# The first piece of q through SyncE's queue in fp32, with a new written-out order, in a fused Nyström attention and feed-forward kernel

## The chip, the cores and the metric

One core of one Trainium2 chip runs the whole program in one launch. The metric is the device time of an execution in microseconds, lower is better. The engines are TensorE (PE, its weight loads PEld), VectorE (DVE), ScalarE (ACT), GpSimd (POOL) and SyncE (SP); DMAs are issued by GpSimd (software queue, q0 in the profile) and by SyncE (hardware queue, q1), and once by ScalarE.

## The reference

```python
# q, k, v: (8, 8, 576, 64) fp32; m = 32 landmarks, scale = 1/8
q_lm = q.reshape(B, H, 32, 18, 64).mean(axis=3)      # and k_lm from k
sm = lambda a, b: softmax(scale * a @ b.T)           # with +1e-9 in the divisor
A, Bm, C = sm(q, k_lm), sm(q_lm, k_lm), sm(q_lm, k)
Z = Bm.T / (norm1(Bm) * norminf(Bm) + 1e-6)          # of each head
for _ in range(6):
    Z = 2 * Z - Z @ Bm @ Z
x = (A @ Z @ C @ v), heads side by side               # (4608, 512)
out = relu(x @ w_in) ** 2 @ w_out                     # w_in 512x2048, w_out 2048x512
```

## The kernel before, in words

The work goes by batch b = 0..7. A batch has two tiles of heads: r = 0 is heads 0 to 3, r = 1 heads 4 to 7, with partition = (head, landmark) and 18 tokens of 64 values along a partition (1152 values). Names of operations end in the batch, then in what they handle: `ldq0.1` loads q of batch 0, heads 4 to 7.

**Loads.** `load_qk` (L411 to L417) issues a DMA from GpSimd that reads fp32 and writes bf16 into the tile X (three buffers). v, w_in and w_out come the same way. All loads are in one software queue, in the order of their words; at most eight are in flight, and GpSimd waits for the eighth last to land before it issues the next. SyncE issues only the stores of the output (L1095).

**Attention of a batch.** `lm` on PE sums the 18 tokens of each landmark (two forms: L492 for heads 0 to 3 of batch 0 and for batch 1, L499 for heads 4 to 7 of batch 0), from X with the identity `ident` as the weight; `lmc`, `lme` bring it into LM, `lmt` transposes. `T` (L461, DVE) transposes X in 32x32 blocks. `B` (L546) is the 32x32 score matrix of the landmarks; `Bmx Bsb Bex Bsu Brc Bml` are its softmax (Bml, L562, multiplies by the reciprocal into Bf), `Bmb` (L580) makes the bf16 copy Bb from the same factors, `Btr` transposes it, `Bcs Bnm Brn` give the norm, `BBT Yi Zi` (L643) start the iteration, `N` (PE) and `U` (DVE, L699) are its six steps. `SC` (L721), `Cmx`, `Cex` (L762), `CT` are C; `CR` gathers its sums through `cpick` (c11). `CV` is C times v (L807), `Zm` and `ZC` multiply by Z, `W` (L878) multiplies by w_in and `We` evicts it. `SA` is A for batches 0 and 1 (L927), whose softmax is `Amx` (L945), `Asb` (L948), `Aex` (L950), `Asu` (L952), `Arc` (L955) and `Aml` (L957, the multiplication by the reciprocal); for batch 0 each is cut in two, a and b. `Ap` transposes on PE and `Ab` evicts. `bk` (L933) spreads k's landmarks for SA.

**Feed-forward.** `F` (L1042) multiplies, `R` applies relu out of PSUM (L1056 on ACT, L1058 on DVE), `Q` squares (L1063 on ACT, L1065 on DVE or GpSimd) into the ring G, `O` (L1082) is the second product, `Oe` evicts and `St` stores.

**What sets the order.** Nothing is scheduled by the compiler: a string `ORDER` lists all 1421 operations by name, with the PSUM bank (`@2`) and, where it isn't the first choice, the engine (`/A` ACT, `/D` DVE, `/P` POOL). A planner (`Plan.schedule`) walks it with a cost for each operation and a free time for each engine (`T0`), a start of the software queue (`SW0`) and a landing delay (`LAND`), and the operations are emitted by planned start. So an engine's instruction order is that of the words given to it. `Plan.fillers` then puts products of constants (`onesb`, L1156) into PE's planned gaps until the first `O0.`, with a rule for how much of each stretch of 3.41 us has to be filled. Their results are not used.

Of the kernel before, what the change touches and what calls it, by code (L numbers as in the profile page):

```python
# [53 lines left out]
class Plan:  # L54
# [104 lines left out]
    def fillers(self, until, width, emit):  # L159
# [3 lines left out]
        for o in ops:  # L163
            a, b = o.start, o.start + o.engs["PE"]
            free = [j for j in range(8)
                    if all(h[1] >= a + 0.15 or h[2] <= at - 0.02 for h in self.history if h[0] == j)]
            if free:
                unit = width if at > 6 else 2 * width
                gaps.append([at, max(0, int((a - 0.05 - at) / unit)), free[0], a, unit])
            kind = o.name.rstrip("0123456789.ab")  # L170
            used.append((a, b, self.USE.get(kind, 0.95)))
            at = max(at, b + 0.04)

        def share(t):
# [12 lines left out]
        for at, n, j, _, unit in gaps:  # L187
# [5 lines left out]
            o.emit = lambda e, j=j, n=n: emit(j, n)  # L193
# [7 lines left out]
T0 = {"PE": 1.1, "ACT": 1.1, "DVE": 1.1, "POOL": 1.31, "SP": 1.1}  # L201
SW0, LAND, LOADED = 1.5, 1.75, 140.0
# [53 lines left out]
def kernel(  # L256
# [155 lines left out]
    def load_qk(b, t, r):  # L412
# [4 lines left out]
           W=[("X", b % 3, t, r)], nbytes=589824, queue="sw")  # L417
# [33 lines left out]
    def attention(b):  # L451
        x, tt, lm, lt = X[b % 3], TT[b % 2], LM[b % 2], LT[b % 2]
        kx = lambda t, r: ("X", b % 3, t, r)
# [5 lines left out]
        def transposes(t):  # L459
            for r in range(2):  # L460
# [3 lines left out]
                   R=[kx(t, r)], W=[kt(t, r)])  # L464
# [19 lines left out]
        def landmarks(rs):  # L484
# [4 lines left out]
            def lmx(e):  # L489
# [14 lines left out]
               R=["ident", *[kx(t, r) for t in range(2) for r in rs]], W=[pl_], alloc=[pl_],  # L504
# [37 lines left out]
        def sB(e):  # L542
# [19 lines left out]
        op(f"Bml{b}", {"DVE": 0.14}, lambda e: nc.vector.tensor_tensor(  # L562
            bf[:], bl[:], bc(s_[:, 4:6]), ALU.mult), R=[kb("bl"), kb("brc")], W=[kb("bf")])
# [15 lines left out]
        else:  # L579
            op(f"Bmb{b}", {"DVE": 0.14}, lambda e: nc.vector.tensor_tensor(  # L580
                bb[:], bl[:], bc(s_[:, 4:6]), ALU.mult), R=[kb("bl"), kb("brc")], W=[kb("bb")])
# [47 lines left out]
        def bbt(e):  # L629
# [281 lines left out]
        for u in range(2) if b in TOKENS else ():  # L911
# [28 lines left out]
            for j, (x0, x1) in enumerate(zip(cuts, cuts[1:])):  # L940
# [11 lines left out]
                op(f"Asu{b}.{u}{z}", {"DVE": v_(w)}, lambda e, s3=s3, sa3=sa3, at=at: nc.vector.tensor_reduce(  # L952
                    s3(1)[:, at], sa3[:, at], axis=AX.X, op=ALU.add), R=kx_("sa"), W=kx_("asu"))
                op(f"Arc{b}.{u}{z}", {"DVE": 0.07 + 0.0045 * (x1 - x0)}, lambda e, s3=s3, at=at:
                   nc.vector.reciprocal(s3(2)[:, at], s3(1)[:, at]), R=kx_("asu"), W=kx_("arc"))  # L955
                op(f"Aml{b}.{u}{z}", {"DVE": v_(w)}, lambda e, sa3=sa3, b3=b3, anv=anv, at=at:
                   nc.vector.tensor_tensor(anv.rearrange("p (x m) -> p x m", m=M)[:, at], sa3[:, at],  # L957
                                           b3(2)[:, at], ALU.mult),
                   R=[*kx_("sa"), *kx_("arc")], W=kx_("An"))
# [216 lines left out]
FLAT_LM = ((0, 0), (1, 0))  # L1176

# [142 lines left out]
```

## Time and profile before

| | |
|---|---|
| median of 3 runs | 264.09 us (263.49 to 264.58) |
| profiled execution | 264.03 us, span 262.3 us |
| instructions in the span | 7508 |
| mean granted TensorE clock | 0.998 |
| HBM read, written | 48.50 MB, 9.44 MB |

The time of an execution is about 1.7 us more than the span of the profile, which begins with the program's first instruction and ends with its last. In the profile "DMA X<-in_q_dram" names the transfer that writes tile X from q. Names of tiles leave out the buffer's number, so every load of q has that name, and they are told apart by their time. A line in brackets after an instruction is the idle time of its engine ahead of it and what ended it.

### The profile page before, as it was taken

The page shows a single profiled execution, that of the slowest core. Times are in us where ns is not written, and L with a number is a line of the kernel's source. Part 1 is how long each engine was busy: PE and PEld are TensorE (multiplying, and loading weights), DVE is VectorE, ACT ScalarE, POOL GpSimd, SP SyncE. Part 2 cuts the span into 40 slices and gives each one's busy share as a digit, 9 for nine tenths or more (in the row PEclk, how much of TensorE's full clock was granted, in tenths as well). Part 3 has the DMA queues.
Part 4 walks back from the last instruction along what each step waited for, and adds up shares of the span by engine and source line. Part 5 has one row for each costly group of instructions (what it writes and reads, how often), then busy time and mean ns, then how long its engine had stood idle before and what let it go on. Part 6 is the DMA issues. An engine that isn't in the chain of part 4 may idle for free.

```text
span 262.3 us, 7508 instructions
## 1 busy us (share of the span) xinstructions
PE 248.2 (95%) x3053; PEld 140.7 (54%) x3092; DVE 208.9 (80%) x551; ACT 184.6 (70%) x334; POOL 70.3 (27%) x114
## 2 busy tenths in 40 slices
PE   7797999999999999999999999899999999999993
PEld 2464566566454656465555456466454655457552
DVE  3899898888999798988998889979998868764110
ACT  1272797866498897898767389888676965699421
POOL 8446486554021442053601411000202010000000
PEclk9999999999999999999999999999999999999999
DMA  6999999999977399689997495360005210060045
GB/s 103 205 187 200 208 207 206 205 210 192 191 153 170 39 223 216 138 117 216 198 188 166 75 223 107 58 152 1 2 0 135 70 42 1 2 152 8 2 115 128
DMA packets 25123, 34.18 MB, mean 130 GB/s; under 512 B 2432, under 2 KB 14464, under 8 KB 25088
## 3 DMA queue, kind: packets, MB, share of 16 engines
q0 software_dynamic: 19168, 24.25, 55.3%
q1 hardware_dynamic: 5840, 9.38, 13.8%
q8 instruction: 24, 0.39, 0.6%
q14 instruction: 11, 0.09, 0.1%
q10 hardware_dynamic: 80, 0.07, 0.1%
HBM read 48.50 MB, written 9.44 MB: 221 GB/s over the span
## 4 chain that ended last, share of the span: by engine, by line
PE 64%; DVE 12%; ACT 8%; DMA 8%; issue 4%; POOL 2%; SPq 2%; POOLq 0%; DVEq 0%; ACTq 0%
PE ps L1082 35%; PE ps L1042 17%; DMA X<-in_q_dram 4%; DMA out_dram<-OS 4%; PE ps L878 3%; ACT RS L1056 2%; ACT G L1063 2%; PE ps L807 2%; SPq L1095 2%; PE ps L721 2%; POOL X L416 1%; DVE RS L1058 1%; DVE An L1012 1%; ACT C L762 1%; PE ps L477 1%
## 5 line engine op out<-in xcount | busy, mean ns | idle before, releaser
L1082 PE MATMUL ps<-w_out,G 128*128 128x512 bf16 (+1 forms) x557 | 133.9, 373 | 2.9 <-issue 1.4
L1082 PEld LDWEIGHTS <-G 128*128 128x128 bf16 x592 | 54.5, 98 | 54.4 <-issue 5.5
L1042 PE MATMUL ps<-AT,WP 128*128 128x288 bf16 (+2 forms) x512 | 74.6, 286 | 0.7 <-DVE RS L1058 0.2
L1056 ACT ACTIVATE RS<-ps 128x576 bf16<-128x576 f32 (+2 forms) x96 | 59.4, 652 | 11.2 <-PE ps L1042 7.3
L1042 PEld LDWEIGHTS <-WP 128*128 128x128 bf16 x512 | 48.1, 98 | 21.3 <-issue 2.9
L1063 ACT ACTIVATE G<-RS 128x576 bf16<-128x576 bf16 (+2 forms) x69 | 46.6, 690 | 4.0 <-DVE RS L1058 3.3
L403 ACT CAST WP<-ps 128x1024 bf16<-128x1024 f32 (+1 forms) x28 | 25.9, 971 | 9.1 <-PE ps L878 9.0
L403 ACT COPY OS<-ps 128x512 f32<-128x512 f32 (+2 forms) x32 | 18.0, 569 | 18.6 <-PE ps L1082 17.6
L1058 DVE TENSOR_SCALAR RS<-ps 128x576 bf16<-128x576 f32 (+2 forms) x32 | 24.1, 754 | 6.3 <-PE ps L1042 4.4
L622 POOL TENSOR_TENSOR BD<-ST,blkb 128x256 bf16<-128x256 bf16 x14 | 9.8, 702 | 68.7 <-DVE ST L699 57.3
L1065 DVE TENSOR_TENSOR G<-RS 128x576 bf16<-128x576 bf16 (+2 forms) x51 | 22.3, 451 | 7.2 <-ACT RS L1056 6.8
L461 DVE STREAM_TRANSPOSE TT<-X 128x576 uint32<-128x576 uint32 x32 | 24.3, 765 | 1.1 <-DMA X<-in_k_dram 0.5
L762 ACT ACTIVATE C<-ps,sm 128x576 bf16<-128x576 f32 x16 | 14.3, 906 | 7.8 <-DVE sm L759 7.8
L699 DVE SCALAR_TENSOR_TENSOR ST<-ST,ps 128x128 bf16<-128x128 bf16 (+1 forms) x48 | 12.8, 267 | 6.9 <-PE ps L685 4.9
L432 POOL DMA_DIRECT2D V<-in_v_dram x24 | 12.8, 534 | 13.3 <-PE ps L807 7.5
L407 DVE COPY OS<-ps 128x512 f32<-128x512 f32 (+1 forms) x6 | 3.8, 625 | 14.1 <-DMA out_dram<-OS 8.7
L1156 PE MATMUL ps<-onesb 128*128 128x512 bf16 (+1 forms) x38 | 11.9, 407 | 2.0 <-DVE onesb L339 1.5
L622 POOL TENSOR_TENSOR BD<-Bt,blkb 128x256 bf16<-128x256 bf16 x4 | 3.1, 770 | 36.6 <-ACT Bt L403 11.0
L759 DVE TENSOR_REDUCE sm<-ps 128x1 f32<-128x576 f32 x16 | 11.6, 745 | 0.7 <-PE ps L721 0.6
L1065 POOL TENSOR_TENSOR G<-RS 128x512 bf16<-128x512 bf16 (+1 forms) x8 | 8.8, 1100 | 7.5 <-ACT RS L1056 7.4
L995 DVE STREAM_TRANSPOSE SA<-ps 128x320 f32<-128x320 f32 (+1 forms) x24 | 10.0, 456 | 0.9 <-PE ps L716 0.7
L878 PE MATMUL ps<-w_in,ZC 64*32 64x512 bf16 x256 | 10.6, 383 | 0.0
(139 smaller groups left out, 299.9 us busy)
## 6 DMA issues: line engine op xcount, KB each, us to landing
out_dram<-OS SPq DMA_DIRECT2D x70, 128.0 KB, 2.4
X<-in_q_dram POOLq DMA_DIRECT2D x16, 288.0 KB, 9.5
X<-in_k_dram POOLq DMA_DIRECT2D x16, 288.0 KB, 8.6
XS<-in_q_dram POOLq DMA_DIRECT2D x5, 576.0 KB, 6.9
XS<-in_k_dram POOLq DMA_DIRECT2D x5, 576.0 KB, 10.4
V<-in_v_dram POOLq DMA_DIRECT2D x8, 288.0 KB, 9.2
w_in<-in_moe_w_in_dram POOLq DMA_DIRECT2D x8, 256.0 KB, 10.5
w_out<-in_moe_w_out_dram POOLq DMA_DIRECT2D x4, 512.0 KB, 9.3
```

Source lines behind the costliest of these rows:

```text
L403: nc.scalar.copy(o, i)
L432: lambda e, r=r, p0=p0, n=n, src=src: nc.gpsimd.dma_start(vv[32 * p0:32 * (p0 + n), r].rearrange("p s d -> p (s d)"), src),
L461: op(f"T{b}.{t}{r}", {"DVE": v_(576)}, lambda e, r=r: nc.vector.transpose(tt[:, t, r].rearrange("p s m e -> p (s m e)").bitcast(U32), x[:, ...
L622: bdiag = lambda e, o, i: eng(e).tensor_tensor(o.rearrange("p r (c m) -> p r c m", c=4), i.unsqueeze(2).to_broadcast([P, 2, 4, M]), blkb[: ...
L762: op(f"Cex{b}.{r}", {"ACT": a_(576) + 0.27}, lambda e, r=r: nc.scalar.activation(Cs[r][:].rearrange("p x u -> p u x"), cbanks(r), AF.Exp, ...
L878: nc.tensor.matmul(ps[quad(pos_a(c, r)), pW.at + r, :], lhsT=zcs[r][half, pos_c(c, r), :], rhs=w_in[half, c, 512 * ch:512 * ch + 512], sta ...
L1042: nc.tensor.matmul(ps[:, ph.at + i, 0:w], lhsT=wp[:, r, 128 * ff:128 * ff + 128], rhs=at[:, r, t0:t0 + w], start=(r == 0), stop=(r == 1))
L1056: nc.scalar.activation(rs, pair(ph, w), AF.Relu)
L1058: nc.vector.tensor_scalar(out=rs, in0=pair(ph, w), scalar1=0.0, scalar2=None, op0=ALU.max)
L1063: nc.scalar.activation(g, rs, AF.Square)
L1065: eng(e).tensor_tensor(g, rs, rs, ALU.mult)
L1082: nc.tensor.matmul(bank(po)[:, 0:c1 - c0], lhsT=G[:, f, lo:lo + P], rhs=w_out[:, f, c0:c1], start=(f == 0), stop=(f == NF - 1))
```

## The change

1. `SYNC = ((0, 0, 1),)`: the piece ldq0.1 (batch 0, q, heads 4 to 7) is loaded by SyncE as fp32 into space of the ring G that isn't used yet, 4608 bytes on each of 128 partitions. Two casts of 576 columns each, cs01.0 on ACT and cs01.1 on DVE, bring it into X. The keys of X become two halves for each piece. All other loads stay in GpSimd's queue.
2. Operations that may run on other engines: Bml, Zi, Blo and the Aml of batches 0 and 1 on GpSimd; Bmb becomes a copy of Bf instead of a second multiplication, and may be on ACT. The new order uses this for Aml0.1a, Aml0.1b, Bml0, Bml7, Zi0 and Zi2 (GpSimd) and for Bmb0 and Bmb1 (ACT).
3. Fillers: the gap that spans `GATE` = 5.1 is cut there, and the products after that point read X (the piece from SyncE) in place of the constants, so they wait for its first half. Ahead of GATE a product counts as twice as long, after it (till 7.0) only 0.55 of the gap is filled.
4. The planner's constants: `T0` of SP 1.1 to 2.9, `SW0` 1.5 to 2.7. They touch nothing but the planned order.
5. The whole order is written anew, 1423 words.

```diff
-                unit = width if at > 6 else 2 * width
-                gaps.append([at, max(0, int((a - 0.05 - at) / unit)), free[0], a, unit])
+                for x, y in ((at, a),) if not at < GATE < a - 0.6 else ((at, GATE), (GATE, a)):
+                    unit = 2 * width if x < GATE else width
+                    n = (y - 0.05 - x) / unit
+                    gaps.append([x, max(0, int(n if x < GATE or x > 7.0 else 0.55 * n)), free[0], y, unit])
...
-T0 = {"PE": 1.1, "ACT": 1.1, "DVE": 1.1, "POOL": 1.31, "SP": 1.1}
-SW0, LAND, LOADED = 1.5, 1.75, 140.0
+T0 = {"PE": 1.1, "ACT": 1.1, "DVE": 1.1, "POOL": 1.31, "SP": 2.9}
+SW0, LAND, LOADED = 2.7, 1.75, 140.0
+GATE = 5.1
...
+    def first(t, r):
+        return G[:, 4 * t + 2 * r:4 * t + 2 * r + 2].rearrange("p f n -> p (f n)").bitcast(F32)
+
+    def load_first(t, r):
+        src = (q, k)[t][0, 4 * r:4 * r + 4].rearrange("c (m s) d -> (c m) (s d)", s=SEG)
+        op(f"ld{'qk'[t]}0.{r}", {"SP": 1.5}, lambda e: nc.sync.dma_start(first(t, r), src), W=[("XF", t, r)])
+        for j in range(2):
+            at = slice(576 * j, 576 * j + 576)
+            op(f"cs{t}{r}.{j}", {"DVE": 0.38, "ACT": 0.59}, lambda e, at=at: copy(
+                e, X[0][:, t, r].rearrange("p s d -> p (s d)")[:, at], first(t, r)[:, at]),
+               R=[("XF", t, r)], W=[("X", 0, t, r, j)])
...
-        op(f"Bml{b}", {"DVE": 0.14}, lambda e: nc.vector.tensor_tensor(
-            bf[:], bl[:], bc(s_[:, 4:6]), ALU.mult), R=[kb("bl"), kb("brc")], W=[kb("bf")])
+        op(f"Bml{b}", {"DVE": 0.14, "POOL": p_(64)}, lambda e: eng(e).tensor_tensor(
+            bf[:], bl[:], bc(s_[:, 4:6]), ALU.mult), R=[kb("bl"), kb("brc")], W=[kb("bf")], port=("POOL",))
...
-            op(f"Bmb{b}", {"DVE": 0.14}, lambda e: nc.vector.tensor_tensor(
-                bb[:], bl[:], bc(s_[:, 4:6]), ALU.mult), R=[kb("bl"), kb("brc")], W=[kb("bb")])
+            op(f"Bmb{b}", {"DVE": 0.14, "ACT": a_(64)}, lambda e: copy(e, bb[:], bf[:]),
+               R=[kb("bf")], W=[kb("bb")])
...
-                op(f"Aml{b}.{u}{z}", {"DVE": v_(w)}, lambda e, sa3=sa3, b3=b3, anv=anv, at=at:
-                   nc.vector.tensor_tensor(anv.rearrange("p (x m) -> p x m", m=M)[:, at], sa3[:, at],
+                op(f"Aml{b}.{u}{z}", {"DVE": v_(w), "POOL": p_(w)}, lambda e, sa3=sa3, b3=b3, anv=anv, at=at:
+                   eng(e).tensor_tensor(anv.rearrange("p (x m) -> p x m", m=M)[:, at], sa3[:, at],
...
-    def fill(j, n):
+    def fill(j, n, late):
+        x = X[0][:, SYNC[0][1], SYNC[0][2]].rearrange("p s d -> p (s d)") if late else onesb
         for w in [512] * (n // 2) + [256] * (n % 2):
-            nc.tensor.matmul(ps[:, j, 0:w], lhsT=onesb[:, 0:P], rhs=onesb[:, 0:w], start=True, stop=True)
+            nc.tensor.matmul(ps[:, j, 0:w], lhsT=onesb[:, 0:P], rhs=x[:, 0:w], start=True, stop=True)
```

The beginning of the order, as far as the first products (before, then after):

```diff
-c0 ldq0.1 c13 c17 ldk0.1 ldq0.0 ldk0.0 ldq1.0 c1 c5 Bce0@0 c2 c3 lm0.1@2 c12 c6 c15 ldk1.0 ldk1.1
-ldq1.1 T0.01 T0.11 lmc0.10/D lmc0.11 c9 lme0.1 lmt0.1 SC0.1@2 win20 ldv0.11 win01 ldv0.00 ldv0.10
-win10 win11 win00 T0.00 c8 Cmx0.1 T0.10 T1.00 lm0.0@1 lme0.0/D lmt0.0 bk0 Cex0.1 c10 B0@4 Bmx0
-CT0.1 Bsb0 Bex0 SC0.0@2 Cmx0.0 Cex0.0 c11 Bsu0 Brc0 SA0.1@6 Amx0.1b Bml0 Bmb0 SA0.0@1 Amx0.0b Btr0
-Amx0.0a Bcs0 Bnm0 Crc0 Asb0.1b Brn0 c14/A Asb0.0b Aex0.0b Cmk0 BBT0@2 Zi0 Yi0 Amx0.1a Asb0.0a
-Asb0.1a lm1.0@5 Aex0.1b lme1.0 N0.0@0 U0.0 N0.1@0 ldq2.1 win30 win31 ldv1.11 lmt1.0 bk1/P B1@2
-Asu0.0b ldq2.0 c18 ldk2.0 ldk2.1 win21 U0.1 N0.2@0 Aex0.1a Asu0.1a CT0.0 Bmx1 U0.2 Bsb1 Asu0.1b
-Bex1 Aex0.0a CR0@4 CRe0/A N0.3@7 U0.3 Bsu1 Arc0.0b Arc0.1a Arc0.1b N0.4@0 U0.4 Brc1 Asu0.0a Bml1
-N0.5@2 Bmb1 U0.5 Arc0.0a Blo1 Aml0.0b Btr1 CV0@4,6 Zd0@2 Zm0 Bcs1@0 Bnm1 CVe0.0/A CVe0.1/A BBT1@3
-ZC0@4 ZCe0 Aml0.0a Ap0.0@0 Ab0.0/A Bad1 T1.01 SA1.1@6 Brn1 Aml0.1b Aml0.1a Yi1 Zi1 T1.11 W0.0@0
+c0 ldk0.1 c1 c5 c12 ldq0.1 cs01.0/A ldq0.0 ldk0.0 c13 c6 c17 Bce0@6 ldq1.0 c2 ldk1.1 ldk1.0 ldq1.1
+c11 c9 cs01.1 c3 lm0.1@0 T0.11 lmc0.10/D lmc0.11 T0.01 lme0.1 lmt0.1 SC0.1@0 win30 ldv0.00 win00
+ldv0.10 ldv0.11 T0.00 Cmx0.1 T0.10 c10 Cex0.1 c15 T1.00 lm0.0@4 lme0.0 lmt0.0 B0@2 c8 bk0 Bmx0
+Bsb0 CT0.1 Bex0 Bsu0 SC0.0@0 Cmx0.0 Brc0 Bml0/P SA0.1@4 Amx0.1b Amx0.1a Bmb0/A Btr0 SA0.0@7
+Amx0.0b Bcs0 Asb0.1a Bnm0 Cex0.0 BBT0@2 Asb0.1b Brn0 Crc0 Yi0 win11 win10 win01 Zi0/P Aex0.1a
+Aex0.1b Cmk0 Amx0.0a Asu0.1b Asb0.0b Arc0.1b win31 ldq2.1 Aml0.1b/P ldk2.0 ldk2.1 win20 c14/A
+lm1.0@3 lme1.0 N0.0@2 U0.0 N0.1@6 lmt1.0 bk1/P ldv1.11 B1@2 win21 ldq2.0 U0.1 Asb0.0a N0.2@6 Bmx1
+Bsb1 U0.2 CT0.0 Asu0.1a Aex0.0b Bex1 CR0@1 N0.3@0 U0.3 N0.4@2 Asu0.0b Bsu1 U0.4 Aex0.0a Arc0.0b
+Brc1 Asu0.0a N0.5@5 U0.5 Arc0.0a Arc0.1a Aml0.1a/P ldv1.00 Bml1 Aml0.0a CRe0/A CV0@6,2 Zd0@0
+Bmb1/A Blo1 Bcs1@5 Zm0 Btr1 CVe0.0/A CVe0.1/A ZC0@4 BBT1@1 ZCe0 Bnm1 Aml0.0b Ap0.0@0 Ab0.0/A Bad1
+T1.01 SA1.1@2 Brn1 Zi1 Yi1 T1.10 T1.11 W0.0@0 We0.01 We0.00 N1.0@4 U1.0 W0.1@6 We0.1 N1.1@4 U1.1
```

In the rest of the order the operations are the same, their places are not. Over all batches these change engine (to the engine on the left of the count): squares Q to DVE 29, from DVE 21; evictions of W to DVE 5, from DVE 3; outputs Oe to DVE 9 (five of them in tiles 27 to 35), from DVE 3; relus R to DVE 19, from DVE 18; the products BD to DVE 12, from DVE 9; ZCe from DVE 4, to DVE 1; lme from DVE 3, to DVE 1.

More of the change, by code (lines that the diff above doesn't have):

```diff
@@ L192, in fillers @@
             o.engs, o.end = {"PE": n * width}, at + n * width
-            o.emit = lambda e, j=j, n=n: emit(j, n)
+            o.emit = lambda e, j=j, n=n, late=at == GATE: emit(j, n, late)
             self.order.insert(next(i for i, x in enumerate(self.order)
@@ L416, in load_qk @@
            lambda e: nc.gpsimd.dma_start(x[:, t, r].rearrange("p s d -> p (s d)"), src),
-           W=[("X", b % 3, t, r)], nbytes=589824, queue="sw")
+           W=[("X", b % 3, t, r, j) for j in range(2)], nbytes=589824, queue="sw")
+    def first(t, r):
[8 more added lines that the diff above has]
+               R=[("XF", t, r)], W=[("X", 0, t, r, j)])
     def load_xs(b):
@@ L452, in attention @@
         x, tt, lm, lt = X[b % 3], TT[b % 2], LM[b % 2], LT[b % 2]
-        kx = lambda t, r: ("X", b % 3, t, r)
+        kx = lambda t, r: [("X", b % 3, t, r, j) for j in range(2)]
         kt = lambda t, r: ("TT", b % 2, t, r)
@@ L596, in attention @@
             else:
-                op(f"Blo{b}", {"DVE": 0.14}, lambda e: nc.vector.tensor_tensor(
-                    blo[:], bf[:], bb[:], ALU.subtract), R=[kb("bf"), kb("bb")], W=[kb("blo")])
+                op(f"Blo{b}", {"DVE": 0.14, "POOL": p_(64)}, lambda e: eng(e).tensor_tensor(
+                    blo[:], bf[:], bb[:], ALU.subtract), R=[kb("bf"), kb("bb")], W=[kb("blo")], port=("POOL",))
                 def bcl(e):
@@ L642, in attention @@
         ks = lambda j: ("ST", i2, j)
-        op(f"Zi{b}", {"DVE": 0.14}, lambda e: nc.vector.tensor_tensor(
+        op(f"Zi{b}", {"DVE": 0.14, "POOL": p_(64)}, lambda e: eng(e).tensor_tensor(
             st[0][:, :, 1, :], bf[:], bc(s_[:, 10:12]), ALU.mult),
-           R=[kb("bf"), kb("rn")], W=[(*ks(0), "z")])
+           R=[kb("bf"), kb("rn")], W=[(*ks(0), "z")], port=("POOL",))
         op(f"Yi{b}", {"DVE": 0.14}, lambda e: nc.vector.tensor_tensor(
@@ L1176 @@
 FLAT_LM = ((0, 0), (1, 0))
+SYNC = ((0, 0, 1),)
 MERGED = (2, 3, 4, 5, 6, 7)
```

190 lines of the change are left out of this document (96 added, 94 removed).

## The prediction, made before the change was run

> **What bounds the kernel now.** First the page and a table of stages. Columns of the table: stretch, its length, busy us of PE, PEld, DVE, ACT and POOL with counts, granted clock, DMA share, GB/s written.
>
> ```profile
> PE 248.2 (95%) x3053; PEld 140.7 (54%) x3092; DVE 208.9 (80%) x551; ACT 184.6 (70%) x334; POOL 70.3 (27%) x114
> ```
> ```profile
> 0.00:15.00 15.00, 11.46 (x145) 6.16 (x147) 9.29 (x28) 3.07 (x8) 8.89 (x22) 1.00 0.89 161
> 15.00:30.00 15.00, 12.92 (x267) 7.66 (x267) 14.41 (x58) 8.33 (x25) 8.43 (x15) 1.00 1.17 195
> 30.00:45.00 15.00, 14.80 (x274) 10.13 (x274) 13.55 (x30) 14.00 (x26) 10.39 (x14) 1.00 1.18 208
> 45.00:250.00 205.00, 201.04 (x2337) 112.48 (x2369) 170.79 (x438) 156.80 (x272) 42.55 (x66) 1.00 0.62 118
> ```
>
> From 45 us on PE is busy 201.04 of 205 us: what reaches PE earlier ends earlier, and little is left to gain there. Before 30 us the first feed-forward product has hardly begun, and DVE is full (14.41 of 15). So a gain has to come from the opening. Its order is in the chain of waits (start, us, what):
>
> ```profile
> 1.30 2.84 POOL X L416 x5
> ...
> 5.99 10.64 DMA X<-in_q_dram
> ...
> 16.77 2.13 PE ps L492 x18
> ...
> 25.38 0.68 DVE TT L461
> ...
> 27.83 0.39 PE ps L878 x8
> ...
> 29.37 0.61 PE ps L1042 x4
> ```
>
> The reader is to see three links: GpSimd issues the eight pieces of q and k of batches 0 and 1; the last, ldq1.1, lands at 5.99 + 10.64 = 16.63 and releases lm1.0 (L492); then DVE carries the chain to T1.01 (25.38); the first w_in product W0.0 (L878) follows, and the first feed-forward product F0.2 stands at 29.37. The change reaches both: a transfer leaves GpSimd's queue, and work leaves DVE.
>
> **The change, part by part.** *1. The piece that changes queues.* When pieces land now (issue time from the timeline, KB and us to landing from the DMA issues of a narrow window):
>
> ```profile
> 2.02 0.54 POOL L416 DMA_DIRECT2D X<-in_k_dram  x1
> ```
> ```profile
> X<-in_k_dram POOLq DMA_DIRECT2D x1, 288.0 KB, 4.9
> ```
>
> ldk0.1 lands at 2.02 + 4.9 = 6.9, ldq1.1 six pieces later at 16.63: 1.62 us a piece. Taking ldq0.1 out moves every later landing up by 1.62 us, less what the same piece takes on SP's queue. There it writes 0.59 MB of fp32 instead of 0.295 of bf16. No load runs on SP's queue now; the nearest rows are the stores, q1, beside the loads, q0 (windows 8:15, 71:74 and 96.5:97.5):
>
> ```profile
> DMA packets 732, 1.45 MB, mean 208 GB/s; under 512 B 79, under 2 KB 129, under 8 KB 731
> ```
> ```profile
> DMA packets 468, 0.78 MB, mean 261 GB/s; under 512 B 64, under 2 KB 134, under 8 KB 467
> ...
> q0 software_dynamic: 237, 0.39, 71.7%
> q1 hardware_dynamic: 230, 0.38, 39.3%
> ```
> ```profile
> DMA packets 229, 0.33 MB, mean 327 GB/s; under 512 B 41, under 2 KB 87, under 8 KB 229
> ...
> q1 hardware_dynamic: 170, 0.28, 76.4%
> q0 software_dynamic: 59, 0.04, 39.5%
> ```
>
> Loads alone write 208 GB/s, 0.62 MB in 3 us; beside 0.38 MB of stores they wrote 0.39. That is 0.23 MB or 1.1 us lost, 1.7 us for 0.59 MB. The third window: 0.208 - 0.04 = 0.17 MB lost for 0.28, again 1.7 us for 0.59. So beside the loads the SP piece would cost all it saves. What it has is a head start. GB/s in 40 slots of 0.1 us, from 0.0 (first load issued at 1.30) and from 80.3 (where the first of a group of stores is issued, its row under the slots):
>
> ```profile
> GB/s 0 0 0 0 0 0 0 0 0 0 0 0 0 0 0 0 0 0 0 0 0 0 0 0 0 0 0 138 115 115 138 161 184 207 161 207 207 161 115 184
> ```
> ```profile
> GB/s 161 23 23 0 0 0 0 0 0 0 0 20 205 307 123 246 143 205 226 184 246 287 82 246 123 226 307 164 184 246 103 205 246 205 246 184 205 103 307 225
> ```
> ```profile
> SPq L1304 <- PEq L1304: 0.7, 1, 0.7
> ```
> ```profile
> 66.06 29.00 SPq L1095 DMA_DIRECT2D out_dram<-OS  x14
> ```
>
> GpSimd's first bytes come at 2.7, a store's 1.2 us after its issue. SP is free from 0.7 and issues nothing before 66.06, so nothing is queued behind or ahead of the load there: issue at about 0.85, bytes at 2.05, 0.65 us ahead. At 0.28 MB per us (third window) 0.18 MB are through by 2.7; the other 0.41 MB cost 1.7 x 0.41 / 0.59 = 1.2 us. **Lead of all later loads: 1.62 - 1.2 = 0.4 us**, an estimate; the ends are 1.62 (it costs the loads nothing) and -0.1 (no head start). The first use is safe: q0.1 is in by about 4.5 (2.7 + 0.41 / 0.28 = 4.2, and some 0.3 till it is told) and has till T0.01 and lm0.1, which wait for ldk0.1 anyhow (6.9 now).
>
> The Trainium skill, "DMA: Bandwidth & Descriptors", section "Issuing engines are not separate DMA queues", speaks against this part: DMAs of all issuing engines run on the same 16 engines and interleave, and several issuers save only sequencer time. By it the lead would be only the head start; the two windows of stores beside loads agree with it (1.7 us for the piece). It is the second rival below, and by it the sum would be the -0.3 given there.
>
> The two casts (ACT and DVE halves) are new. The nearest rows, of a transpose and of a smaller cast:
>
> ```profile
> 6.89 0.78 DVE L461 STREAM_TRANSPOSE TT<-X 128x576 uint32<-128x576 uint32 x1 [0.53 <-DMA X<-in_k_dram]
> ...
> 17.75 0.41 ACT L403 CAST dupm<-identf 128x256 bf16<-128x256 f32 x1
> ```
>
> 0.41 us for 256 columns makes some 0.8 for 576 (the transpose of 576 took 0.78), on ACT and DVE at once, from 4.5 to 5.3: ahead of k, where ACT has 3.07 of 15 us and DVE idles 0.53 us waiting, so 0. Behind the cast that waits stand on DVE c3 (the identity that lm0.1 needs, so at 5.5, and k comes later still) and on ACT c11 and c10, wanted only from the masks of C on. Without that cover (q0.1 later than 6) it is 0.8. The fillers that read X wait for the ACT half; behind them on PE stands lm0.1, which waits for k: 0, again unless q is late. T0.01 goes behind T0.11: up to 0.78 on lme0.1, whose cover is that k0.0 and then q1.1 come later still.
>
> *2. DVE between lm1.0 and T1.01.*
>
> ```profile
> 15.47 0.21 DVE L562 TENSOR_TENSOR Bf<-Bl,sm 128x64 f32<-128x64 f32 x1
> ...
> 15.60 0.22 DVE L580 TENSOR_TENSOR Bb<-Bl,sm 128x64 bf16<-128x64 f32 x1
> ...
> 18.26 0.81 DVE L948 TENSOR_TENSOR SA<-ps,smA 128x256 f32<-128x256 f32 x2
> ...
> 21.36 0.46 DVE L952 TENSOR_REDUCE smA<-SA 128x10 f32<-128x320 f32 x1
> ...
> 22.07 0.34 DVE L955 RECIPROCAL smA<-smA 128x8 f32<-128x8 f32 x3
> ...
> 22.32 1.17 POOL L933 TENSOR_TENSOR BK<-LT,blkw 128x512 bf16<-128x512 bf16 x1
> ...
> 22.96 0.62 DVE L562 TENSOR_TENSOR Bf<-Bl,sm 128x64 f32<-128x64 f32 x1
> ...
> 26.04 0.86 DVE L957 TENSOR_TENSOR An<-SA,smA 128x320 bf16<-128x320 f32 x2
> ```
>
> By the two orders, Asu0.1b (0.46), Arc0.1b (a third of 0.34) and Bmb1 (as Bmb0, 0.22) leave the stretch and Asb0.0a (half of 0.81) enters it: **-0.38 us**. Ahead of lm1.0 DVE loses Bml0, Bmb0, Zi0 (0.21, 0.22 and one of the same shape), lme0.0 and Asb0.0a, and gets Asu0.1b and Arc0.1b: some 0.6 us less, so it is ready for an lm1.0 that comes 0.4 earlier. The ends are 0 (another engine ends the wait) and -1.0 (both cuts on the path). The path Bml0 (GpSimd), Bmb0 (ACT), Btr0 has two more changes of engine; hidden because N0.0 stands behind lm1.0 on PE; uncovered, by two hand-overs of the 0.14 that lm1.0 took from landing (16.63) to start, 0.3.
>
> *What is late next* is w_in, which W0.0 waits for:
>
> ```profile
> 16.91 0.61 POOL L440 DMA_DIRECT2D w_in<-in_moe_w_in_dram  x1 [1.41 <-DMA X<-in_q_dram]
> ```
> ```profile
> w_in<-in_moe_w_in_dram POOLq DMA_DIRECT2D x1, 256.0 KB, 9.7
> ```
>
> The last piece that W0.0 needs lands at 16.91 + 9.7 = 26.6, 1.2 us ahead of W0.0 (27.83). In the new order win01 is that piece, with the same loads ahead of it but ldq0.1, so at 26.2 with the lead of 0.4; W0.0 would be at 27.0. The cut of DVE is not taken back there, up to 1.2 us of it.
>
> *3. A's last products on GpSimd.* Both Aml0.1 (0.86 us of DVE at 26.04, after T1.01) go to GpSimd; from BK, 1.17 us for 512 columns, about 0.75 each. Behind them on GpSimd stand ldk2.0 and ldv1.00, DMAs that take some 10 us to land because the queue is full, so a wait of 1 us is hidden. DVE is freed of 0.86 us where the stage 30:45 has it at 13.55 of 15 but ACT at 14.00: I take a quarter, **-0.2**; ends 0 and -0.86. Against it: Bml1 took 0.62 instead of 0.21 beside GpSimd's BK and ended with it. That price of 0.4 now falls beside Aml0.1a instead of bk1: no net.
>
> The Trainium skill, "SBUF — State Buffer", section "SBUF: two separate sides", has this as an exclusive lock: a DVE operation with two SBUF inputs and a GpSimd operation block each other for the whole instruction. The trace agrees (0.62 against 0.21). By it each product moved to GpSimd can hold DVE up for the rest of its 0.75, and this part would be +0.4 at worst instead of -0.2.
>
> *4. The rest of the order.* Words of batches 1 to 7 change engine. Net to DVE: 8 squares, 2 W evictions, 1 each of output and relu, 3 small ones, less 3 ZC evictions and 2 landmarks. The rows of 45:250:
>
> ```profile
> L1065 DVE TENSOR_TENSOR G<-RS 128x576 bf16<-128x576 bf16 x45 | 19.7, 451 | 7.2 <-ACT RS L1056 6.8
> L407 DVE CAST WP<-ps 128x1024 bf16<-128x1024 f32 x4 | 4.9, 1220 | 1.4 <-PE ps L878 1.3
> ```
>
> 8 x 0.45 + 2.5 x 1.2 + some 0.8 = **7.4 us more on DVE**, about as much less on ACT. DVE has 34 us free there, so I take 0 for it; the upper end is in the last rival, the lower (ACT freed where it is the bound) -0.5.
>
> **Sum**: -0.4 - 0.38 - 0.2 = -1.0 us. The profiled execution took 264.03 us (span 262.3 and 1.7 around it), the median is 264.09: no difference worth a term. **Forecast 263.0.**
>
> **Rivals.** *The lead is whole* (0.24): SP's piece moves where GpSimd's stream leaves room, and POOL's relief is kept: -1.62 - 0.38 - 0.5 = 261.5. For it: the loads write 208 GB/s, mixed windows 261 to 327 in all, so there is room. Against: the loads' loss of 1.7 us above.
> *The change doesn't do what it says* (0.13): shared engines eat the lead, ldq1.1 lands at 16.6 as now, and the DVE cut alone remains, -0.3: 263.7.
> *DVE becomes the bound* (0.23), the slower one. Stretches where DVE is full now:
>
> ```profile
> 65.00:80.00 15.00, 14.78 (x183) 7.34 (x184) 14.66 (x41) 11.32 (x22) 2.41 (x4) 1.00 1.00 176
> 155.00:170.00 15.00, 14.13 (x215) 8.39 (x217) 14.54 (x42) 13.69 (x26) 1.21 (x2) 1.00 0.56 107
> ```
>
> If 40% of the 7.4 us fall into such stretches, 3.0 us are lost: 263.0 + 3.0 = 266.0. It decides from 2.35 us (32%).
>
> **Chances.** Forecast 0.40, rivals 0.24, 0.13, 0.23. A measurement tells about 0.5% from no change, 262.8 to 265.4. Faster: the whole lead and a third of the forecast's spread, 0.36. Slower: the last, 0.23. Same: 0.41. Range 261.2 to 266.3: the whole lead with 0.3 of the freed ACT, up to 45% of the DVE work in full stretches.
>
> **What would show it.** Step 1: ldk0.1 lands near 6.5 and lm1.0 starts at 16.4 (whole lead: 15.2; none: 16.8). Step 2 and 3: F0.2 between 28.2 and 28.8. Step 4: PE's share in 65:80 and 155:170 as now, DVE's idle not gone. Wrong it would be if q's piece lands after 6 (PE idle ahead of lm0.1), or if the stretches after 45 us grow.

## The result and the profile after

The changed kernel takes 266.14 us (median of 22 runs, 264.87 to 267.52), the kernel before beside it 264.48 (22 runs): a ratio of 1.0055, 95% interval 1.0034 to 1.0076, so slower by 0.55%. The profiled execution took 266.55 us with a span of 264.8. The forecast was 263.0, a gain; the time lies in the stated range, but on the other side of the kernel before.

The busy line of the page after, and the table of stages (columns as in the prediction):

```profile
PE 249.6 (94%) x3049; PEld 141.1 (53%) x3088; DVE 216.5 (82%) x560; ACT 178.2 (67%) x325; POOL 68.7 (26%) x115
```
```profile
0.00:15.00 15.00, 11.54 (x130) 5.85 (x132) 8.59 (x25) 5.66 (x17) 7.58 (x19) 1.00 0.92 182
15.00:30.00 15.00, 13.24 (x270) 8.11 (x270) 14.34 (x54) 6.76 (x20) 10.35 (x17) 1.00 1.17 204
30.00:45.00 15.00, 14.49 (x274) 9.67 (x273) 13.50 (x28) 13.38 (x25) 12.04 (x16) 1.00 1.14 186
45.00:250.00 205.00, 199.84 (x2329) 111.88 (x2361) 176.74 (x450) 152.13 (x264) 38.73 (x64) 1.00 0.63 120
```

DVE gained 7.6 us in all (208.9 to 216.5) and ACT lost 6.4; between 45 and 250 us DVE gained 5.95 (170.79 to 176.74), where the prediction counted 7.4. Nearly all of that lies late, where it cost PE nothing. From 200 to 250 us, before and after:

```profile
200.00:250.00 50.00, 49.46 (x420) 28.14 (x425) 31.07 (x66) 36.53 (x61) 2.00 (x3) 1.00 0.22 50
200.00:250.00 50.00, 49.45 (x453) 28.20 (x460) 36.94 (x81) 33.97 (x57) 0.67 (x1) 1.00 0.23 54
```

The opening did not shorten: F0.2, 29.37 before, starts here at 29.87.

```profile
29.87 0.60 PE L1061 MATMUL ps<-AT,WP 128*128 128x256 bf16 x4
```

The rest grew: from F0.2 to the last instruction it takes 234.9 us (264.8 - 29.87), in the kernel before 232.9 (262.3 - 29.37). So there are two questions: where the forecast gain of the opening went, and what takes the 2.0 us later. The timeline of the changed kernel shows two new waits of PE, both ahead of a first product of W from ZC. The first:

```profile
44.59 0.64 DVE L971 TENSOR_REDUCE smA<-SA 128x16 f32<-128x512 f32 x1
...
44.87 1.04 POOL L1084 TENSOR_TENSOR G<-RS 128x512 bf16<-128x512 bf16 x1 [0.51 <-ACT RS L1075]
45.16 1.10 DVE L1084 TENSOR_TENSOR G<-RS 128x640 bf16<-128x640 bf16 x1
...
46.35 0.60 ACT L1075 ACTIVATE RS<-ps 128x512 bf16<-128x512 f32 x1 [1.56 <-DVE G L1084]
...
46.98 0.43 DVE L1084 TENSOR_TENSOR G<-RS 128x512 bf16<-128x512 bf16 x1 [0.56 <-ACT RS L1075]
47.00 0.41 PE L897 MATMUL ps<-w_in,ZC 64*32 64x512 bf16 x8 [0.63 <-ACT RS L1075]
```

Read it from below. W1.1 (47.00) needs the PSUM bank that F0.8 holds; the relu R0.8 on ACT frees it (46.35) and had waited 1.56 us with ACT idle, because it writes the buffer RS that the square Q0.18 still reads. That square now stands on DVE, behind the sum Asu1.0 (44.59), and took 1.10 us for 640 columns beside a square on GpSimd (44.87, 1.04 us), where one of 512, with no square on GpSimd beside it, took 0.43 (46.98). In the kernel before the same square ran on ACT at 43.67, and W1.1 started without a wait:

```profile
43.67 0.74 ACT L1063 ACTIVATE G<-RS 128x640 bf16<-128x640 bf16 x1
...
45.32 0.41 PE L878 MATMUL ps<-w_in,ZC 64*32 64x512 bf16 x8
```

The second wait, in the changed kernel:

```profile
110.22 0.22 DVE L577 TENSOR_REDUCE sm<-Bl 128x2 f32<-128x64 f32 x1 [0.32 <-ACT Bl L575]
...
110.56 0.74 DVE L1077 TENSOR_SCALAR RS<-ps 128x576 bf16<-128x576 f32 x1
...
111.35 0.41 PE L897 MATMUL ps<-w_in,ZC 64*32 64x512 bf16 x8 [0.52 <-DVE RS L1077]
```

Here the relu R2.15, moved from ACT to DVE, stands behind a softmax step that waits for ACT, and W3.2 waits for its bank. 0.63 + 0.52 = 1.15 us of PE.

The stretches that the prediction named for its slower rival do not show a loss; PE's share there rose (14.78 to 14.89, 14.13 to 14.61):

```profile
65.00:80.00 15.00, 14.89 (x141) 7.84 (x143) 13.40 (x37) 11.64 (x21) 7.57 (x14) 1.00 1.00 163
155.00:170.00 15.00, 14.61 (x200) 8.59 (x206) 14.73 (x43) 12.26 (x25) 0.00 (x0) 1.00 0.63 126
```

### The profile page after: what moved, and what is told of

The parts are those of the page before. It is cut to its first block, busy times and chain, and to the rows that moved or that the text cites. A ratio compares the mean times of both kernels' runs of the same rounds, so it can differ in the third digit from the quotient of the medians.

```text
span 264.8 us, 7515 instructions
## 1 busy us (share of the span) xinstructions
PE 249.6 (94%) x3049; PEld 141.1 (53%) x3088; DVE 216.5 (82%) x560; ACT 178.2 (67%) x325; POOL 68.7 (26%) x115
## 4 chain that ended last, share of the span: by engine, by line
PE 56%; DVE 29%; ACT 8%; issue 3%; DMA 2%; DVEq 0%; ACTq 0%; POOLq 0%
PE ps L1101 29%; PE ps L1061 16%; DVE G L1084 3%; DVE RS L1077 3%; PE ps L897 3%; ACT RS L1075 3%; DVE TT L480 2%; ACT C L781 2%; DMA X<-in_k_dram 2%; DVE An L1031 2%; DVE sm L778 2%; DVE smA L1025 2%; ACT G L1082 2%; DVE ZM L860 1%; DVE SA L1014 1%
## 5 line engine op out<-in xcount | busy, mean ns | idle before, releaser
L1082 ACT ACTIVATE G<-RS 128x576 bf16<-128x576 bf16 (+2 forms) x62 | 41.8, 688 | 5.5 <-DVE RS L1077 4.8
L1084 DVE TENSOR_TENSOR G<-RS 128x576 bf16<-128x576 bf16 (+2 forms) x59 | 27.2, 472 | 6.6 <-ACT RS L1075 6.2
L410 ACT COPY OS<-ps 128x512 f32<-128x512 f32 (+1 forms) x26 | 14.6, 571 | 19.7 <-PE ps L1101 19.7
L641 POOL TENSOR_TENSOR BD<-ST,blkb 128x256 bf16<-128x256 bf16 x12 | 8.5, 704 | 70.6 <-DVE ST L718 57.1
L410 ACT CAST WP<-ps 128x1024 bf16<-128x1024 f32 (+1 forms) x26 | 23.7, 949 | 4.1 <-PE ps L897 2.4
L480 DVE STREAM_TRANSPOSE TT<-X 128x576 uint32<-128x576 uint32 x32 | 24.2, 760 | 2.0 <-DMA X<-in_k_dram 2.0
L414 DVE COPY OS<-ps 128x512 f32<-128x512 f32 (+2 forms) x12 | 7.5, 631 | 8.8 <-PE ps L1101 5.6
L1176 PE MATMUL ps<-onesb 128*128 128x512 bf16 (+1 forms) x33 | 11.0, 413 | 2.2 <-DVE onesb L346 1.5
L1025 DVE TENSOR_REDUCE smA<-SA 128x20 f32<-128x640 f32 (+1 forms) x12 | 8.7, 738 | 2.9 <-ACT SA L1023 2.9
L704 PEld LDWEIGHTS <-BD 128*128 128x128 bf16 x72 | 6.5, 98 | 7.3 <-DVE BD L641 1.2
```

The costliest lines, as they stand in the source:

```text
L410: nc.scalar.copy(o, i)
L480: op(f"T{b}.{t}{r}", {"DVE": v_(576)}, lambda e, r=r: nc.vector.transpose(tt[:, t, r].rearrange("p s m e -> p (s m e)").bitcast(U32), x[:, ...
L1025: op(f"Asu{b}.{u}", {"DVE": v_(nn)}, lambda e, sa=sa, sx=sx: nc.vector.tensor_reduce(sx[:, 1].rearrange("p r s -> p (r s)"), fl(sa), axis= ...
L1082: nc.scalar.activation(g, rs, AF.Square)
L1084: eng(e).tensor_tensor(g, rs, rs, ALU.mult)
```

## The experiments

A second suspect was the clock. In the profile after, the early products of constants and the first landmark product lm0.1 (L518) run at half speed until about 11 us, where the kernel before is at full speed from 5.2 (lm0.1 took 0.70 us there):

```profile
7.03 1.18 PE L518 MATMUL ps<-X,ident 64*64 64x128 bf16 x36 [0.94 <-DMA X<-in_k_dram]
8.14 1.03 PE L1176 MATMUL ps<-onesb 128*128 128x512 bf16 x2
```

The first four trials set this clock theory against the order theory (the new order of the later batches costs by itself) and try the SyncE load alone. Ratios are to the kernel before, timed beside the trials: 264.89 us beside the first four of the table, 264.81 beside the next four, 264.56 beside the three after them, 264.36 beside the last. The kernel before itself thus differs by half a us between these times.

| trial | us | ratio (95%) |
|---|---|---|
| changed kernel, earlier rule for early products | 268.33 | 1.0143 (1.0090 to 1.0196) |
| changed kernel, twelve early products | 266.66 | 1.0069 (1.0044 to 1.0093) |
| before, five early products | 265.48 | 1.0016 (0.9986 to 1.0046) |
| before with SyncE's load | 267.23 | 1.0076 (1.0044 to 1.0109) |
| new opening, old rest | 265.19 | 1.0020 (0.9997 to 1.0043) |
| old opening, new rest | 266.50 | 1.0073 (1.0045 to 1.0100) |
| before, Aml0.1 on GpSimd | 264.23 | 0.9977 (0.9955 to 1.0000) |
| changed kernel without SyncE's load | 268.55 | 1.0142 (1.0105 to 1.0178) |
| changed kernel, two operations back | 264.50 | 1.0010 (0.9990 to 1.0029) |
| before, the same two moved | 266.42 | 1.0064 (1.0040 to 1.0089) |
| before, Aml0.1 on GpSimd, more products near 25 us | 264.80 | 1.0013 (0.9996 to 1.0029) |
| changed kernel, the square back | 264.89 | 1.0012 (0.9984 to 1.0040) |

**Twelve early products in the changed kernel** (none reads q's piece, and PE is busy until 0.85 us before lm0.1; the other products follow the earlier rule, whose lines are left out of the diff):

```diff
-        x = X[0][...] if late else onesb
+        x = onesb
...
+            n = 24 if at < 5.5 < y else n
```

> The changed kernel with twelve early products of constants of 512 columns after Bce0, none reading q's piece, so that PE is busy until the landmarks' data land. Clock theory: first record of the clock near 5 to 6 us, lm0.1 in 0.70 us, SC0.1 near 9.2, F0.2 at 28.8 to 29.1 (changed kernel 29.9), time 264.8 to 265.1, about 1.2 below the changed kernel and no slower than 0.3% above the kernel before. Order theory: F0.2 near 29 all the same, but the later stretches take it back or keep their 1 to 2 us, time 265.6 to 266.3.

```profile
7.58 0.70 PE L517 MATMUL ps<-X,ident 64*64 64x128 bf16 x36 [0.85 <-DMA X<-in_k_dram]
...
29.42 0.60 PE L1060 MATMUL ps<-AT,WP 128*128 128x256 bf16 x4
```

The clock is full ahead of lm0.1 (0.70 us) and F0.2 starts 0.45 sooner than in the profile of the changed kernel, and that one execution is 0.48 us shorter (266.07 against 266.55). But the median is 266.66, no better than 266.14: a full clock there does not bring the loss back.

**Five early products in the kernel before** (`n = 10 if at < 5.5 < y else n`, so PE idles from 4.6 us to 7.1):

> The kernel before with one thing changed: five instead of ten and a half early products of 512 columns after Bce0, so PE idles from about 4 us until the landmarks' data land at 6.9. Clock theory: the clock opens only after 8 us, lm0.1 takes 1.1 us instead of 0.70, SC0.1 starts 0.6 to 1.0 us later, F0.2 0.3 to 0.8 later, time 265.0 to 265.8 against 264.5. Order theory: 264.3 to 264.7, no change.

265.48, a ratio whose interval goes from -0.4 to +1.2 us: it holds no change and most of what the clock theory forecast, so this trial does not decide. Nor did the clock do what was expected: in the profile lm0.1 still took 0.70 us, PE was at half speed from 8.5 to 11.9 us, and F0.2 started at 29.95, 0.58 later than before.

**The changed kernel with the earlier rule for early products:**

> The changed kernel with the earlier rule for the early products of constants: none of them reads q's first piece, so after Bce0 five of 512 columns run without a pause instead of 2.5, a wait and 2. Clock theory (the opening loses because PE's clock opens at 11.0 us instead of 5.2): the pause is gone, but PE still idles ahead of lm0.1, so part comes back; if the clock opens ahead of lm0.1, lm0.1 takes 0.70 us instead of 1.18, F0.2 starts by 29.0 and the time falls by 1.0 to 1.3 us, to about 265.0; if the stretch of products is too short to open it, 266.1 as the changed kernel. Order theory (the new order of batches 1 to 7 is worse by itself): 265.8 to 266.3 whatever the clock does.

268.33, outside both expectations, and here the clock does show. In a window at 27 us of this profile (the columns as above; the third number from the end is the granted clock):

```profile
27.00:30.40 3.40, 2.92 (x39) 1.76 (x39) 2.60 (x8) 0.83 (x2) 0.60 (x1) 0.54 1.12 206
```

The clock was at half for 3.4 us from 27.3 on, with W0.0 (29.45) inside. The rule decides how many products of constants stand between 8 and 25 us, but that too few of them cost the clock is not shown: from 24.0 to 27.4 us PE was busy 2.34 us here and 2.27 in the kernel before, which kept it.

**The kernel before with SyncE's load** (and the two casts ahead of lm0.1, in the changed kernel's code; no other word moved):

```diff
-c0 ldq0.1 c13 c17 ldk0.1 ... c2 c3 lm0.1@2
+c0 c13 c17 ldq0.1 ldk0.1 ... c2 c3 cs01.0/A cs01.1 lm0.1@2
```

> The kernel before with the first piece of q by SyncE's queue and the two casts, nothing else moved; early products as before (one and ten and a half). Lead theory: the later pieces land 0.2 to 0.85 us sooner (q1.1 at about 15.8 instead of 16.6) and lm1.0 starts sooner, but DVE carries the chain to T1.01; time 264.0 to 264.4, a gain of 0.1 to 0.5. Rival (w_in and DVE end the opening anyway): 264.5, no change. Second rival (casts and the cold clock cost): 264.8 to 265.5.

```profile
8.29 0.70 PE L517 MATMUL ps<-X,ident 64*64 64x128 bf16 x36 [1.35 <-DMA X<-in_k_dram]
```
```profile
27.00:30.40 3.40, 2.97 (x20) 1.98 (x20) 2.09 (x7) 0.85 (x2) 1.30 (x3) 0.57 1.21 209
```

Slower, by none of the ways expected: k's first piece landed only at 8.15 (6.87 before), the last piece of q at 17.86 (16.63 before), and the clock fell near 27 us as in the trial above. How much of the loss is the load's and how much the clock's, this trial doesn't tell.

**The two halves exchanged.** But for three words, the orders hold the same operations up to `wout3` (some 40 us), so they can be cut there: the new opening with the old rest, and the old opening (all loads on GpSimd's queue) with the new rest, whose banks are renamed.

> The changed kernel's code and its order up to wout3 (about 40 us: SyncE's load, the casts, A's products on GpSimd, the early products), and from there the order of the kernel before. Order theory (the new order after the opening is what costs): PE's two new waits for ZC (46.4 and 110.8 us, 0.63 and 0.52 us) are gone and the time is 1.0 to 2.0 us below the changed kernel's 266.1, so 264.2 to 265.1. Opening theory: 265.8 to 266.4, as the changed kernel.

> The reverse: the opening of the kernel before up to wout3 (all pieces on GpSimd's queue, A's products on DVE, its early products), and from there the changed kernel's order. Order theory: F0.2 starts at 29.4 as before, the two waits for ZC are there, and the time is 1.2 to 2.0 us above before's 264.9, so 266.1 to 266.9. Opening theory: 264.6 to 265.2.

265.19 and 266.50: the loss is in the rest of the order. With the old opening F0.2 starts at 29.07, 0.3 sooner than before, and PE still waits ahead of the same two products of W, 0.64 us at 45.3 and 0.52 at 110.1. The new opening brings no gain that can be told (1.0020, 0.9997 to 1.0043).

The profiles agree. From F0.2 to the last instruction all five with the new rest as it stands take 234.9 to 235.3 us, though F0.2 starts between 29.07 and 32.79 in them. The kernel before and three trials with its rest take 232.7 to 233.1. Two more with that rest take longer: five early products (234.8), and the new opening with the old rest (234.2), where PE waits 1.2 us behind an eviction that itself waits 2.04 us for a store.

**Two operations back on ACT**, in their places:

```diff
-Q0.18
+Q0.18/A
...
-R2.15/D
+R2.15
```

> The changed kernel with two operations back on ACT, in the same places of the order: the square Q0.18 and the relu R2.15, which the change had put on DVE. Theory (PE's two new waits of 0.63 and 0.52 us come from these two on DVE's queue: the late square keeps a buffer that ACT's relu needs, the late relu keeps a PSUM bank that W3.2 needs): both waits go, and the time falls by 0.6 to 1.2 us below the changed kernel's 266.1, to 264.9 to 265.5. Rival (ACT, given back 1.4 us, becomes late instead, or the next wait takes it back): 265.8 to 266.4.

```profile
44.18 0.73 ACT L1082 ACTIVATE G<-RS 128x640 bf16<-128x640 bf16 x1
...
44.94 0.60 ACT L1075 ACTIVATE RS<-ps 128x512 bf16<-128x512 f32 x1
...
45.80 0.41 PE L897 MATMUL ps<-w_in,ZC 64*32 64x512 bf16 x8
```
```profile
108.68 0.63 ACT L1075 ACTIVATE RS<-ps 128x576 bf16<-128x576 f32 x1
108.80 0.98 PE L897 MATMUL ps<-w_in,ZC 64*32 64x512 bf16 x24
```

Both waits are gone, all of W3's products run without a break, and the time is 264.50, level with the kernel before (264.56). Two words of some 1400 hold all of the loss that can be told (the interval leaves -0.3 to +0.8 us). This profile has the half-speed opening too (lm0.1 takes 1.18 us), so that opening is not what the changed kernel loses. From F0.2 to the end it takes 233.5 us, 1.5 less than the changed kernel.

**The same two moved in the kernel before** (`Q0.18/A` to `Q0.18`, `R2.15` to `R2.15/D`):

> The reverse in the kernel before: Q0.18 and R2.15 moved from ACT to DVE, nothing else. If it is the move itself that costs, 0.4 to 1.2 us over before, 265.2 to 266.0; if the waits need the other changes of order around them too, 264.6 to 265.1, no difference.

266.42, more than expected, and through another wait: in the profile the square costs PE nothing, the relu 1.31 us. The trial's rows, then those of the kernel before:

```profile
105.23 0.76 DVE L1058 TENSOR_SCALAR RS<-ps 128x576 bf16<-128x576 f32 x1 [0.50 <-ACT G L1063]
...
106.27 0.81 DVE L1006 TENSOR_REDUCE smA<-SA 128x20 f32<-128x640 f32 x1
...
108.67 0.24 PE L546 MATMUL ps<-LT 32*32 32x32 bf16 x16 [1.31 <-DVE LT L530]
```
```profile
104.97 0.81 DVE L1006 TENSOR_REDUCE smA<-SA 128x20 f32<-128x640 f32 x1
...
107.38 0.24 PE L546 MATMUL ps<-LT 32*32 32x32 bf16 x16
```

The relu waits 0.50 us for its buffer and takes 0.76, and DVE's whole queue behind it, down to the transpose that B5 (L546) needs, is 1.3 us later. A word of 0.76 us costs PE 1.31; the other 0.4 us of the loss of 1.7 (0.0064 of 264.56; 1.1 to 2.4) is not explained.

**The square alone back:**

> The changed kernel with only the square Q0.18 back on ACT; the relu R2.15 stays on DVE. By the two waits of PE the square is worth 0.63 of 1.15 us; both together brought 1.6. If each is worth its wait: 265.4 to 265.6. If the relu is the larger part, as in the kernel before, where its wait was 1.31 us and the square cost nothing: 265.7 to 266.1. If the square is nearly all: 264.5 to 265.0.

264.89 (1.0012): of the 1.66 us that the changed kernel loses, the square is worth about 1.1 by the medians and the relu the rest, but the interval (-0.4 to +1.1 us over the kernel before) leaves the split open. The profile keeps only the second wait, 0.51 us, and takes 234.1 us from F0.2 to the end: 0.8 less than the changed kernel for the square, and 0.6 more than with both back for the relu.

**Both Aml0.1 on GpSimd in the kernel before:**

> The kernel before with both Aml0.1 on GpSimd and nothing else changed. The prediction's step: DVE is freed of 0.86 us ahead of W0.0's evictions, F0.2 0.2 us sooner or as now, time 264.5 to 264.9 (before 264.9). Rival (the products on GpSimd come late or hold DVE up): Ap0.1 or F0.2 later by 0.4 to 0.8, 265.3 to 265.7.

264.23, a ratio of 0.9977: the only version whose interval puts it ahead of the kernel before, and its end touches 1.0000; among twelve trials one such can be chance. F0.2 starts 0.35 sooner than before, but it does so too (29.07) in the trial with the old opening and A's products on DVE, so a single profile doesn't show that it is the products' doing:

```profile
29.02 0.61 PE L1042 MATMUL ps<-AT,WP 128*128 128x256 bf16 x4
```

**The same with 1.3 us more products of constants near 25 us** (`n += 3 * (24.5 < at < 25.5) if n else 0`), to keep the clock there:

> The kernel before with both Aml0.1 on GpSimd (as the earlier trial, 264.23) and 1.3 us more of products of constants in PE's gaps near 25 us, where PE is busy only 2.2 of 3.4 us and some runs lose the full clock. If that loss is what separates the runs (263.9 at a clock of 0.996 and more, 264.4 below), the median falls to 263.7 to 264.0; if the products come in the way of Ap0.0 instead, 264.3 to 264.9.

264.80: no gain; in its profile the clock is at half from 26.9 us to 30.3 all the same.

**The changed kernel without SyncE's load** (the first piece of q second on GpSimd's queue):

> The changed kernel's order with the first piece of q on GpSimd's queue again (no casts, no product reads it). Lead theory: what SyncE's load gave (q1.1 landing at 15.8 instead of 16.6, w_in's last needed piece with it) is lost: q1.1 near 16.6, F0.2 0.3 to 0.8 later than with the load, time 266.4 to 267.0. Rival (the load brings nothing by the end, as the same load cost the kernel before 1.2 us in the trial before): 265.4 to 266.2.

268.55. q's first piece lands at 8.08 us and lm0.1 waits for it, q1.1 lands at 17.07 instead of 15.78, and the clock is at half from 29.4 to 32.8 us, so more than the load is lost. What the load is worth by itself stays open: both trials on it (this and the one in the kernel before) also lost the clock for 3.4 us between 27 and 33 us.

## Why the prediction was wrong, step by step

**What bounds the kernel**: right. PE from 45 us on: with the new rest the end follows F0.2 by 234.9 to 235.3 us, however late F0.2 is.

**Step 1, a lead of 0.4 us: right in size as far as the scatter tells, wrong in worth.** The price was well put: by 4.4 us GpSimd's queue had moved 0.04 MB, against 0.27 before, and 0.23 MB at 208 GB/s are 1.1 us, where 1.2 was forecast. q1.1 lands 10.3 us after its issue at 5.46, at 15.8 instead of 16.63; over six profiles with SyncE's load in the new opening its landing is 15.78 to 16.63, mean 16.07, over six with the old opening 15.49 to 16.88, mean 16.41: 0.34 us, with a scatter as large. ldk0.1 came at 6.99, not 6.5 (6.87 before). The casts were costed at 0, and that holds (q's piece lands at 4.33). But lm1.0 does not start when q1.1 lands:

```profile
5.46 0.56 POOL L423 DMA_DIRECT2D X<-in_q_dram  x1
...
16.54 0.43 PE L610 MATMUL ps<-Bf,blkf 128*128 128x64 f32 x2 [0.37 <-POOL Bf L581]
...
17.10 0.22 PE L655 MATMUL ps<-Bt 32*32 32x32 bf16 x8
17.25 0.50 PE L511 MATMUL ps<-X,ident 128*128 128x256 bf16 x3
```
```profile
X<-in_q_dram POOLq DMA_DIRECT2D x1, 288.0 KB, 10.3
```

On PE's queue lm1.0 (L511) stands behind Bcs0 (L610) and BBT0 (L655), which wait for batch 0's own softmax. That chain, which passes through GpSimd for Bml0, is late here:

```profile
16.20 0.29 POOL L581 TENSOR_TENSOR Bf<-Bl,sm 128x64 f32<-128x64 f32 x1 [3.81 <-DVE sm L579]
16.66 1.91 POOL L459 DMA_DIRECT2D w_in<-in_moe_w_in_dram  x3 [0.17 <-issue]
```

So lm1.0 started at 17.25 (16.77 before, forecast 16.4). The prediction asked "what is late next" and named w_in; next were the products already queued ahead of lm1.0, which it had not listed. Passing through GpSimd is not what made the chain late: with the square back, whose opening is word for word the same but whose clock opened sooner (lm0.1 in 0.70 us), Bcs0 starts at 15.66 and lm1.0 waits for q1.1 again. The half-speed products ahead are the likely cause. The loads of w_in stand behind Bml0 too and are issued at 16.66, after GpSimd had waited 3.81 us; that cost nothing, for the last piece that W0.0 needs landed at 25.27, forecast 26.2, and W0.0 started at 28.21.

The Trainium skill, "DMA: Bandwidth & Descriptors", section "Issuing engines are not separate DMA queues", was weighed as a rival: several issuers share the engines, so only the head start is left. The mean lead of 0.34 us is nearer to that than to a whole piece's 1.62. The forecast's 0.4 had itself been worked out as that head start, so the rule spoke for the forecast and not for the second rival, whose sum is 263.7 with the cut of 0.38 and not with the -0.3 that stands there.

**Step 2, -0.38 on DVE: wrong.** From the start of lm1.0 to that of T1.01 the six profiles with the new opening take 8.6 to 9.6 us (mean 9.0), the six with the old one 8.2 to 8.6 (mean 8.4). The stretch grew; what held DVE up in the changed kernel is shown under step 3.

**Step 3, -0.2: not refuted, but its price was left out.** In the kernel before, the products on GpSimd brought -0.6 us (interval -1.2 to 0), which holds the forecast and also nothing. The Trainium skill, "SBUF — State Buffer", section "SBUF: two separate sides", warned of the lock between DVE and GpSimd. In that trial it fell on nothing; in the changed kernel it did. Bad1 (L632) ended only with Aml0.1a on GpSimd, and T1.01 (L480) behind it came late. The rows of the changed kernel, then those with the two operations back, whose instructions are the same up to here:

```profile
25.82 1.08 DVE L632 TENSOR_SCALAR sm<-sm 128x2 f32<-128x2 f32 x1
26.12 0.74 POOL L976 TENSOR_TENSOR An<-SA,smA 128x320 bf16<-128x320 f32 x1
26.81 0.77 DVE L480 STREAM_TRANSPOSE TT<-X 128x576 uint32<-128x576 uint32 x1
```
```profile
25.81 0.16 DVE L632 TENSOR_SCALAR sm<-sm 128x2 f32<-128x2 f32 x1
25.88 0.78 DVE L480 STREAM_TRANSPOSE TT<-X 128x576 uint32<-128x576 uint32 x1
```

Bad1 took 0.9 us longer, W0.0 started 0.49 later (28.21 against 27.72) and F0.2 0.54 later (29.87 against 29.33). Beside Aml0.1a a DVE operation was held up in four of the six profiles with the new opening, by 0.3 to 0.9 us: the +0.4 "at worst" was not the worst. The moved square agrees with the lock too, 1.10 us beside GpSimd's, where 0.43 x 640 / 512 = 0.54 was to be expected.

**Step 4 is the step that failed: "DVE has 34 us free there, so I take 0 for it".** The new rest behind the old opening cost 1.9 us (0.0073 of 264.81; by its interval 1.2 to 2.6), and two words of it are all of the loss that can be told. DVE's free time is a sum over 205 us, and the sum didn't matter: of the 5.95 us that DVE gained there, 5.87 lie between 200 and 250 us, where PE lost nothing. The two operations were put on DVE where its queue was full or waited, and each held a resource that PE's next product needed: an RS buffer, a PSUM bank. The rival "DVE becomes the bound" had the right engine and sign, but not the mechanism or the place: no loss grows with the busy time in full stretches (65 to 80 and 155 to 170 us are as good as before); two waits at 46 and 111 us make it, and 3.0 us for it were twice the price. That its 266.0 is so near 266.14 is luck: it is the opening's gain of 1.0, which did not come, and a doubled price, and the two errors cancel. Of the prediction's own signs, "if the stretches after 45 us grow" was the one that came true.

**Sum.** Forecast -1.0 + 0; the opening brought no gain that can be told (-0.1 to +1.1 us), and the order cost 1.5 to 1.9 us, which the two words give back.

## What to carry to other kernels

Moving an operation to an engine that is idle "on average" is priced by its place: list what stands ahead of it on the new engine, and which buffer or bank it holds while it waits; a square of 0.74 us on ACT cost about 1.1 us here, a relu of 0.74 to 0.76 us 0.5 of PE in one order and 1.3 in the other, while 5.9 us of added work late in the program cost nothing. When a transfer is made earlier, look at the queue of the engine that uses it: what stands ahead of its first consumer sets the start. In a long hand-written order, a cut where both orders have issued the same operations lets the halves be exchanged, and two trials tell which half loses. Timing a profile from its first feed-forward product to its end does the same without a trial.

## What was not expected of the hardware

The clock in the opening differs between executions of the same instructions. Two kernels with the same opening, word for word, up to 40 us: the changed one (first row) and the one with the square back (the other two):

```profile
L1176 PE MATMUL ps<-onesb 128*128 128x512 bf16 x3 | 1.7, 623 | 0.2 <-issue 0.2
```
```profile
L1176 PE MATMUL ps<-onesb 128*128 128x512 bf16 x5 | 1.4, 383 | 0.0
L518 PE MATMUL ps<-X,ident 64*64 64x128 bf16 x36 | 0.7, 218 | 1.6 <-DMA X<-in_k_dram 1.6
```
```profile
28.47 0.61 PE L1061 MATMUL ps<-AT,WP 128*128 128x256 bf16 x4
```

Between 5.2 and 11 us a product of 512 columns takes 623 ns in the one and 383 in the other, lm0.1 1.18 and 0.70 us, and F0.2 starts at 29.87 and 28.47. Not all of these 1.4 us are the clock's: with two operations back the clock opens as late (lm0.1 1.18 us) and F0.2 starts at 29.33. A single profile of an opening can thus be off by more than a us. The Trainium skill, "TensorE: Matmul & The Clock Gate", Part 1, says that the window that opens the clock runs freely and so differs from run to run. The traces agree that it differs, but by far more than the 500 ns either way that the page gives for back-to-back products: full speed came at 5 us in the one and 11 in the other.

A load on SyncE's queue all but shut GpSimd's out for a while. Between 1.0 and 4.4 us of the changed kernel (q1 is SyncE's queue) GpSimd's moved 0.04 MB, where it moved 0.27 in the kernel before:

```profile
q1 hardware_dynamic: 144, 0.59, 49.4%
q0 software_dynamic: 19, 0.04, 24.6%
```
